# Reordering the first batches of a planned attention-and-FFN kernel: tiles A and B of the first batch ahead, the second batch's hold moved, the planner's transfer costs changed

## The chip, the cores and the metric

The kernel runs on one core of one Trainium2 chip. The core has TensorE (PE in the profile; PEld is its weight load), VectorE (DVE), ScalarE (ACT), GpSimd (POOL) and SyncE (SP), and 16 DMA engines. Each engine works through its own list of instructions strictly in order and waits on semaphores; SP and POOL also issue transfers from their lists. The metric is device time in microseconds, the median of the runs shown. Lower is better.

## The reference

Eight batches of eight heads, 576 queries, 576 keys plus 16 beacon keys that every query sees, 64 values per head. Causal attention is followed by a gated feed-forward network over the 4608 tokens:

```python
B, H, S, Nb, D = (8, 8, 576, 16, 64);  n_tokens, d_model, d_ff = (4608, 512, 1536)
k_all = concatenate([beacon_k, k], axis=2);  v_all = concatenate([beacon_v, v], axis=2)
scores = matmul(q, k_all.T) / sqrt(D)           # -1e9 where key > query; beacons always seen
a = exp(scores - scores.max(-1));  a /= a.sum(-1) + 1e-09
x = matmul(a, v_all)                            # to [B*S, H*D] = [4608, 512]
out = (maximum(x @ w_gate, 0) * (x @ w_val)) @ w_out
```

## The kernel before, in words

**A plan written out by a scheduler.** The program first makes a list of tasks (`add`), each with the engines that may do it, a cost in microseconds, the tasks it depends on, the buffers it holds (`Hold`) and a priority. `Plan.order` then plays the list through once: at every step it takes the task that can begin first, the smaller priority number winning among equals, and writes it behind the others on its engine. The result is a fixed order of instructions for each of the five engines. The costs are constants in the file: `c_dve`, `c_act`, `c_pool`, `c_pe` for the engines; for a transfer, an issue time and a time on "the wire", which is one common resource, and a fixed time behind it until it counts as landed (1.9). A different constant therefore changes no instruction by itself, but may change every order. The chip then runs these orders with its real durations, and an engine whose next instruction is not ready waits, whatever stands behind it.

**Fillers.** Where the plan sees TensorE idle before 160 us, it puts in matmuls that compute nothing (`fill`, line 987), one for each 0.1375 us of the gap (0.275 in the first ten microseconds; after 36 us only where a PSUM bank is free). They are part of TensorE's order for good.

**Attention.** Queries are cut into tiles of 64. For each batch, loads of q and k (lines 551, 576, 604) land in one of eight stage tiles `st`; they are rounded to bf16 `h` (line 511, on POOL or DVE for the first batch, on POOL for the others), turned by TensorE (line 522) and copied to kT and qT (lines 460, 462). v is loaded (lines 638 to 641) and copied to bf16 (line 464 or 462). A *quad* is four heads: its scores (line 740) go to PSUM, DVE adds the mask and takes the minimum of the negated scores (line 688), ACT does the exponential with its sum (line 695), DVE the reciprocal (line 701), POOL the normalisation (line 706). Then the probabilities are turned, for the first batch by TensorE (line 816), later by a DMA transpose (line 826), and multiplied with v (line 836). Query tiles are grouped in A, B (tiles 0 to 3 with their keys, 240 tokens), C, D, E (the other 320 tokens) and F (the last 16 tokens of all heads, lines 790 and 859). For the first batch A and B are a quad step of their own: their probabilities and the turned ones live in a part of the tile xT that is not yet needed, so in the profile the exponential and normalisation of A and B have the output `xT`, the others `pb`. The FFN can begin on the first 240 tokens when A and B of all eight heads are done.

**FFN.** Token spans of 240, 336, seven times 512, and 448. For each of twelve column blocks: four gate matmuls (line 897), ReLU on ACT (line 908), four value matmuls (line 902), product on DVE (line 913); then the output matmuls (line 928) by token tiles of 128, copied out of PSUM by DVE or ACT (460, 462) and stored by SP (line 942). At the end of the last span stands a tile of 64 tokens. It is computed as two column halves, the left on partitions 0 to 63 and the right on 64 to 127 **of the same PSUM bank**; the left half is copied by DVE or ACT and stored by SP, the right half copied and stored by ACT.

**Weights.** Nine transfers (three of w_gate, three of w_val, three of w_out), issued by POOL, each 4 x 128 rows by 512 columns, cast to bf16 on the way (line 474).

**What sets the order around the change.** The priorities: weights have -15, the loads of the first batch -20 (prio in `new_batch`), those of the second `RANK1`; the quads of the first batch 0 to 6, with `AB_FIRST` taken off for its A and B quads. `HELD` makes the loads of a batch, from a given place on, wait until a given weight transfer has been issued: a memset of one element on POOL (line 532) stands for the wait. Place 0 of the second batch is its rest rows of k, place 2 the first head pair's k, place 4 the second pair's.

## Time and profile before

| | us |
|---|---|
| median of 3 runs | 406.01 (405.50 to 406.61) |
| the profiled execution, its own time | 406.85 |
| its span | 404.8 |
| FFN matmuls, lines 897, 902, 928, busy | 104.7, 106.1, 99.1 |
| POOL normalisation, line 706, 272 | 142.1 |
| ACT exponential, line 695, 272 | 144.2 |
| DVE minimum, line 688, 288 | 134.3 |
| share of the 16 DMA engines: SP's queue, POOL's weights | 73.6%, 7.6% |

How to read it: busy times of lines add up per engine, and consecutive matmuls overlap in the records, so a line's sum may exceed its share of the time. A timeline row is start, duration, engine, line, operation, output and inputs, and in brackets the idle time of the engine just before and what ended it. A wait's row names who waited for whom. The share of the DMA engines can exceed 1 where their packets overlap. Times on POOL are rough.

### The profile page before, as it was taken

The numbers are of one execution on the slowest core, as the hardware profiler recorded it, in microseconds if no ns is written. First come the engines' busy times: TensorE is split into PE (matmuls) and PEld (weight loads), VectorE is DVE, ScalarE is ACT, GpSimd is POOL, SyncE is SP. The second block draws the span as 40 slices with busy tenths as digits, with TensorE's granted clock in tenths as the row PEclk, the third lists the DMA queues.
The fourth block names the chain that finished last, engine by engine and source line by source line (L and its number), as shares of the span: only waits on it lengthen the run. The fifth ranks groups of instructions, "written<-read, shape, count | busy, mean of one in ns | idle before, by whom it ended". The sixth has DMA issues, their size and how long they took to land.

```text
span 404.8 us, 9950 instructions
## 1 busy us (share of the span) xinstructions
PE 390.3 (96%) x3276; PEld 206.8 (51%) x3320; DVE 293.9 (73%) x1051; ACT 260.1 (64%) x809; POOL 234.7 (58%) x452
## 2 busy tenths in 40 slices
PE   7999999999999999999999899999999999999995
PEld 4667854655444545544455445454444454444542
DVE  3899798986977997769888977698777733442432
ACT  2989689768786786777776777588757721330320
POOL 6799779947395977567785768577565420000000
PEclk9999999999999999999999999999999999999999
DMA  7999997999999999959999999699948273001102
GB/s 179 215 193 216 240 223 147 185 206 204 203 202 217 236 187 275 185 161 189 254 181 201 228 230 177 171 255 226 172 78 175 42 147 123 0 0 53 52 2 91
DMA packets 174147, 67.99 MB, mean 168 GB/s; under 512 B 146384, under 2 KB 169552, under 8 KB 174096
## 3 DMA queue, kind: packets, MB, share of 16 engines
q1 hardware_dynamic: 169264, 62.57, 73.6%
q0 software_dynamic: 4752, 4.72, 7.6%
q8 instruction: 26, 0.43, 0.4%
q14 instruction: 25, 0.20, 0.2%
q10 hardware_dynamic: 80, 0.07, 0.1%
HBM read 38.54 MB, written 9.44 MB: 119 GB/s over the span
## 4 chain that ended last, share of the span: by engine, by line
PE 85%; DMA 5%; POOL 4%; DVE 2%; issue 2%; ACT 1%; SPq 1%; POOLq 0%; ACTq 0%; DVEq 0%
PE f L928 23%; PE f L902 22%; PE f L897 21%; PE f L740 6%; PE f L836 6%; PE f L522 4%; DMA wo_r<-in_moe_w_out_dram 2%; POOL xT L706 2%; DMA st<-in_v_dram 2%; PE f L816 1%; POOL pb L706 1%; PE f L987 1%; DMA st<-in_beacon_k_dram 1%; PE f L859 1%; PE f L790 1%
## 5 line engine op out<-in xcount | busy, mean ns | idle before, releaser
L706 POOL TENSOR_SCALAR pb<-pb,small 128x320 bf16<-128x320 bf16 (+8 forms) x272 | 142.1, 540 | 78.4 <-DVE small L701 73.5
L695 ACT ACTIVATE pb<-f,small 128x320 bf16<-128x320 f32 (+8 forms) x272 | 144.2, 553 | 22.7 <-DVE small L688 13.7
L688 DVE CUSTOM_DVE_ANT_0 f<-f,mask 128x320 f32<-128x320 f32 (+8 forms) x288 | 134.3, 517 | 12.1 <-PE f L740 7.2
L902 PE MATMUL f<-xT,wv_r 128*128 128x512 bf16 (+3 forms) x470 | 106.1, 358 | 0.5
L908 ACT ACTIVATE g<-f 128x512 f32<-128x512 f32 (+3 forms) x120 | 66.7, 565 | 60.6 <-PE f L897 53.8
L897 PE MATMUL f<-xT,wg_r 128*128 128x512 bf16 (+3 forms) x463 | 104.7, 357 | 0.9
L913 DVE TENSOR_TENSOR hT<-g,f 128x512 bf16<-128x512 f32 (+3 forms) x120 | 75.2, 632 | 38.1 <-PE f L902 34.7
L928 PE MATMUL f<-wo_r,hT 128*128 128x512 bf16 (+2 forms) x439 | 99.1, 374 | 1.9 <-issue 1.0
L897 PEld LDWEIGHTS <-wg_r 128*128 128x128 bf16 x480 | 45.3, 98 | 43.1 <-issue 1.2
L928 PEld LDWEIGHTS <-hT 128*128 128x128 bf16 (+2 forms) x456 | 41.9, 100 | 48.1 <-issue 4.0
L902 PEld LDWEIGHTS <-wv_r 128*128 128x128 bf16 x480 | 44.2, 98 | 42.3 <-issue 2.3
L695 ACT ACTIVATION_READ_ACCUMULATOR pb<-f,small 128x1 f32 x272 | 60.5, 222 | 0.0
L511 POOL TENSOR_SCALAR h<-st 128x512 bf16<-128x512 f32 (+1 forms) x92 | 48.6, 543 | 7.6 <-DMA st<-in_k_dram 3.1
L688 DVE DVE_READ_ACCUMULATOR2_ANT small<- 128x1 f32 x296 | 42.4, 143 | 0.2 <-issue 0.2
L740 PE MATMUL f<-kT,qT 64*64 64x64 bf16 (+7 forms) x640 | 35.9, 295 | 1.5 <-ACT pb L695 1.0
L462 DVE COPY osb<-f 128x512 f32<-128x512 f32 (+2 forms) x26 | 17.7, 681 | 24.0 <-PE f L928 24.0
L701 DVE RECIPROCAL small<-small 128x2 f32<-128x2 f32 (+3 forms) x144 | 22.1, 163 | 14.1 <-ACT pb L695 9.3
L522 PE MATMUL f<-ident,h 128*128 128x128 bf16 (+1 forms) x320 | 27.9, 219 | 2.5 <-POOL h L511 1.4
L522 PEld LDWEIGHTS <-h 128*128 128x128 bf16 (+1 forms) x320 | 21.0, 99 | 15.6 <-POOL h L511 5.8
L740 PEld LDWEIGHTS <-qT 64*64 64x64 bf16 x640 | 15.1, 106 | 23.9 <-issue 18.5
L836 PE MATMUL f<-pTb,v 128*64 128x320 bf16 (+3 forms) x488 | 26.0, 253 | 0.0
L836 PEld LDWEIGHTS <-v 128*64 128x64 bf16 (+1 forms) x512 | 20.6, 109 | 9.7 <-issue 7.2
(60 smaller groups left out, 236.0 us busy)
## 6 DMA issues: line engine op xcount, KB each, us to landing
out_dram<-osb SPq DMA_DIRECT2D x34, 256.0 KB, 2.2
st<-in_k_dram SPq DMA_DIRECT2D x32, 256.0 KB, 4.6
st<-in_q_dram SPq DMA_DIRECT2D x32, 256.0 KB, 5.1
st<-in_v_dram SPq DMA_DIRECT2D x24, 256.0 KB, 5.8
st<-in_v_dram SPq DMA_DIRECT2D x8, 224.0 KB, 6.3
wg_r<-in_moe_w_gate_dram POOLq DMA_DIRECT2D x3, 512.0 KB, 6.2
wv_r<-in_moe_w_val_dram POOLq DMA_DIRECT2D x3, 512.0 KB, 6.6
wo_r<-in_moe_w_out_dram POOLq DMA_DIRECT2D x3, 512.0 KB, 7.7
```

The source lines that it names most:

```text
L511: (nc.gpsimd if x.engine == "POOL" else nc.vector).tensor_scalar(to, src, by, 1.0, ALU.mult, ALU.mult)
L522: nc.tensor.matmul(to, h16.tile[:rows, a * P:(a + 1) * P], ident[:rows, :rows], start=True, stop=True)
L688: nc.vector.tensor_tensor_reduce(out=view(i, n - m), in0=view(i, n - m), in1=msk, scale=1.0, scalar=at(7) if m < n else 3.0e38, op0=ALU.ad ...
L695: nc.scalar.activation(ph.tile.rearrange("p a n -> p (a n)")[:, a:a + n], view(i), AF.Exp, bias=at(i), scale=-1.0, accum_out=at(4 + i))
L706: nc.gpsimd.tensor_scalar(one, one, at(8 + i), 1.0, ALU.mult, ALU.mult)
L740: nc.tensor.matmul(banks[k][b_].tile[64 * i:64 * i + 64, off:off + n], t.q.tile[r, 2 * g + i, 64 * j:64 * j + 64], t.kT.tile[r, 2 * g + i, ...
L836: nc.tensor.matmul(ps.tile[64 * hh:64 * hh + 64, d0:d0 + w], t.v.tile[:rows, c, D * h:D * h + D], rhs(64 * hh), start=(c == 0), stop=(c == ...
L897: nc.tensor.matmul(psg.tile[:, :mt], wg_r[:, ki, nf * P:(nf + 1) * P], xT[:, ki, m0:m0 + mt], start=(ki == 0), stop=(ki == KM - 1))
L902: nc.tensor.matmul(psv.tile[:, :mt], wv_r[:, ki, nf * P:(nf + 1) * P], xT[:, ki, m0:m0 + mt], start=(ki == 0), stop=(ki == KM - 1))
L908: r = add("ACT", c_act(mt), lambda _, psg=psg, g=g: nc.scalar.activation(g.tile[:, :mt], psg.tile[:, :mt], AF.Relu), (a,), (psg, g), -1000 ...
L913: hid.append(add("DVE", c_dve(mt), lambda _, psv=psv, g=g, nf=nf: nc.vector.tensor_mul(hT[nf].tile[:, :mt], g.tile[:, :mt], psv.tile[:, :m ...
L928: nc.tensor.matmul(ps.tile[64 * c:64 * c + rows, :w], hT[nf].tile[:, t0:t0 + rows], wo_r[:, nf, w * c:w * c + w], start=(nf == 0), stop=(n ...
```

## The change

It touches constants of the plan and one detail of the last tile.

- `AB_FIRST` 40 instead of 0: the A and B quads of the first batch get priorities of -40 to -38 instead of 0 to 2.
- `RANK1` -14 instead of -19: the priority of the second batch's loads.
- `HELD`: the second batch's first place is no longer held; its third place (first head pair) waits for the first transfer of w_val instead of the third of w_gate; its fifth place waits for the third of w_val as before.
- The planner's cost of a weight on the wire is 0.70 instead of 0.78 per 128 x 512 block, of v 1.25 instead of 1.54, and the time to landing 1.8 instead of 1.9.
- The last tile's two halves each hold a PSUM bank.

```diff
-RANK1 = -19.0
+RANK1 = -14.0
-HELD = {(1, 0): ("v", 0, 0), (1, 2): ("g", 0, 1024), (1, 4): ("v", 0, 1024)}
+HELD = {(1, 2): ("v", 0, 0), (1, 4): ("v", 0, 1024)}
-AB_FIRST = 0
+AB_FIRST = 40
+W_MOVE = 0.7
+V_MOVE = 1.25
+LAND = 1.8
...
-                end = max(wire, free[e]) + 1.9
+                end = max(wire, free[e]) + LAND
...
-                    end = wire + 1.9
+                    end = wire + LAND
...
-            d[...], s[...]), (), (), work, 0.1, move=0.78 * kos * w / 512,
+            d[...], s[...]), (), (), work, 0.1, move=W_MOVE * kos * w / 512,
...
-            ld = add("DMA", (1.1 if c == 0 else 0.55, 1.54 * rows / P), fetch, (held,), (st,), prio[0])
+            ld = add("DMA", (1.1 if c == 0 else 0.55, V_MOVE * rows / P), fetch, (held,), (st,), prio[0])
...
-            ps, osb = Hold(f_s, 4 if halves == 1 else 3), [Hold(osb_s, 2) for _ in range(halves)]
+            ps, osb = [Hold(f_s, 4 if halves == 1 else 2) for _ in range(halves)], [Hold(osb_s, 2) for _ in range(halves)]
...
-                            nc.tensor.matmul(ps.tile[64 * c:64 * c + rows, :w], hT[nf].tile[:, t0:t0 + rows],
+                            nc.tensor.matmul(ps[c].tile[64 * c:64 * c + rows, :w], hT[nf].tile[:, t0:t0 + rows],
...
-                ev = add("ACT" if c else ("ACT", "DVE"), {...}, evict, (prev,), (ps, osb[c]), -1000 + prio)
+                ev = add("ACT" if c else ("ACT", "DVE"), {...}, evict, (prev,), (ps[c], osb[c]), -1000 + prio)
```

What the built programs then issue, engine by engine, is the same work in another order. POOL's list from the fifth cast to the sixth weight, in words (line numbers of before; "norm AB" is line 706 with output xT, "norm C.." with output pb):

```
before                                   after
cast h (k, second quad, first half)      cast h (same)
cast h (q, same)                         weight wg 1
cast v0, cast v1                         cast v0, cast v1, cast h (k, first quad, second half)
norm AB x6                               norm AB x16
weight wg 1
norm AB x2, cast v2
weight wv 1                              weight wv 1
norm AB x1, memset (hold), norm AB x7    weight wg 2, memset (hold)
norm C.. x1, weight wg 2                 norm C.. x2, weight wv 2
norm C.. x4, weight wv 2                 cast h (k rest, second batch), norm C.. x3, weight wg 3
norm C.. x5, weight wg 3                 norm C.. x2, weight wv 3
```

TensorE's list (matmuls of each kind ahead of the place named):

| ahead of | fillers | turns, line 522 | scores, line 740 | gate, value |
|---|---|---|---|---|
| first gate matmul, before | 76 | 40 | 52 | 0, 0 |
| first gate matmul, after | 62 | 40 | 44 | 0, 0 |
| first value matmul, before | 82 | 40 | 56 | 12, 0 |
| first value matmul, after | 74 | 44 | 48 | 12, 0 |
| first gate matmul of the third span, before | 103 | 108 | 200 | 96, 96 |
| first gate matmul of the third span, after | 91 | 124 | 200 | 96, 96 |

No filler stands behind the last place in either. At the last place all other kinds are equal.

More of the change, by code (lines that the diff above doesn't have):

```diff
@@ L474, in weight @@
         x = add("POOL", W_ISSUE, lambda t: nc.gpsimd.dma_start(
-            d[:, ko:ko + kos, n0:n0 + w], s[:, ko:ko + kos, n0:n0 + w]), (), (), work, 0.1, move=0.78 * kos * w / 512,
+            d[:, ko:ko + kos, n0:n0 + w], s[:, ko:ko + kos, n0:n0 + w]), (), (), work, 0.1, move=W_MOVE * kos * w / 512,
             after=W0 + W_STEP * len(weight_in) / KM)
@@ L933, in ffn, with evict @@
                     need += hid[:11]
-                prev = add("PE", k * c_pe(w) + SWITCH * (halves - 1), outp, need, (ps,) + tuple(hT[k * part:k * part + k]),
+                prev = add("PE", k * c_pe(w) + SWITCH * (halves - 1), outp, need, tuple(ps) + tuple(hT[k * part:k * part + k]),
                            prio + 0.3 + 0.01 * part - (0.5 if part else 0))
             for c in range(halves):
-                def evict(x, c=c, ps=ps, osb=osb[c], rows=rows, w=w):
+                def evict(x, c=c, ps=ps[c], osb=osb[c], rows=rows, w=w):
                     copy(x.engine, osb.tile[64 * c:64 * c + rows, :w], ps.tile[64 * c:64 * c + rows, :w])
@@ L942, in store @@
                     q_.dma_start(out[m0 + t0:m0 + t0 + rows, w * c:w * c + w], osb.tile[64 * c:64 * c + rows, :w])
-                ev = add("ACT" if c else ("ACT", "DVE"), {"ACT": c_act(w), "DVE": c_dve(w)}, evict, (prev,), (ps, osb[c]), -1000 + prio)
+                ev = add("ACT" if c else ("ACT", "DVE"), {"ACT": c_act(w), "DVE": c_dve(w)}, evict, (prev,), (ps[c], osb[c]), -1000 + prio)
                 add("DMA", (0.4, 0.78 / halves), store, (ev,), (osb[c],), prio + OUT)
```

## The prediction

> **What bounds the kernel now.** I read, in this order, the busy time of each engine and the slices, the waits of TensorE, its timeline up to the first FFN matmuls, GpSimd's timeline over the same stretch, the landing times of the transfers, and the last six microseconds.
>
> ```profile
> PE 390.3 (96%) x3276; PEld 206.8 (51%) x3320; DVE 293.9 (73%) x1051; ACT 260.1 (64%) x809; POOL 234.7 (58%) x452
> ...
> PEclk9999999999999999999999999999999999999999
> ...
> L987 PE MATMUL f<-mask,ident x103: 269/273/421, 2.0 to 93.3; 128*128 128x256 bf16 x103
> ```
>
> TensorE is busy 390.3 of 404.8 us. The fourteen idle ones are 2.9 in the first five microseconds, about four behind the last matmul, and some seven between. So the total work of TensorE sets the end, and the useful part of it is the same in both kernels. What can change is the fillers (103 matmuls of line 987, all of them dummies), the waits, and the tail. The waits that the profile can name are few (what waited, for whom; us in total, times, longest):
>
> ```profile
> PE f L740 <- ACT pb L695: 1.0, 2, 0.8
> PE f L522 <- ACT pb L695: 1.0, 1, 1.0
> ...
> PE f L928 <- DMA wo_r<-in_moe_w_out_dram: 0.3, 1, 0.3
> ```
>
> The opening stage is a different matter. There GpSimd is the engine without a pause, and weights are issued between its normalisations:
>
> ```profile
> 11.11 0.62 POOL L464 TENSOR_SCALAR v<-st 128x512 bf16<-128x512 f32 x1 [1.12 <-DMA st<-in_v_dram]
> ...
> 13.73 2.85 POOL L706 TENSOR_SCALAR xT<-xT,small 128x64 bf16<-128x64 bf16 x6 [0.97 <-DVE small L701]
> 16.52 0.94 POOL L474 DMA_DIRECT2D wg_r<-in_moe_w_gate_dram  x1
> 17.50 0.93 POOL L706 TENSOR_SCALAR xT<-xT,small 128x256 bf16<-128x256 bf16 x2
> ...
> 18.98 0.79 POOL L474 DMA_DIRECT2D wv_r<-in_moe_w_val_dram  x1
> 19.82 0.55 POOL L706 TENSOR_SCALAR xT<-xT,small 128x64 bf16<-128x64 bf16 x1
> ...
> 20.39 2.98 POOL L706 TENSOR_SCALAR xT<-xT,small 128x64 bf16<-128x64 bf16 x7
> ```
>
> ```profile
> 25.45 0.58 PE L897 MATMUL f<-xT,wg_r 128*128 128x240 bf16 x4
> ...
> 27.94 1.39 PE L902 MATMUL f<-xT,wv_r 128*128 128x240 bf16 x12
> ```
>
> Start, duration, instruction, and in brackets what it waited for. The sixteen normalisations of A and B (output xT) take 2.85 + 0.93 + 0.55 + 2.98 = 7.3 us but run from 13.7 to 23.4, since two weight issues and a cast of v stand among them. The gate matmuls follow at 25.45, the value matmuls at 27.94. The end:
>
> ```profile
> 400.55 0.42 DVE L462 COPY osb<-f 64x256 f32<-64x256 f32 x1 [0.74 <-PE f L928]
> 401.00 0.37 ACT L460 COPY osb<-f 64x256 f32<-64x256 f32 x1 [9.87 <-DVE osb L462]
> 401.40 0.56 ACTq L942 DMA_DIRECT2D out_dram<-osb  x1
> ```
>
> ScalarE's copy of the last tile's right half starts only when VectorE's copy of the left half, out of the same bank, is done.
>
> **The change, part by part.** *New constants (W_MOVE, V_MOVE, LAND, AB_FIRST, RANK1)* issue nothing by themselves; they re-sort all five queues. What they do is read from the order of the built programs.
>
> *Fillers.* 91 instead of 103. Up to the first gate matmul there are 62 instead of 76, with 8 score matmuls less as well; from there to the end 29 instead of 27. Fourteen of them in a row took 1.70 us (from 11.61), the last one's latency included, so 0.11 us each: 12 x 0.11 = 1.3 us off the engine that sets the end. **-1.3**.
>
> *Last tile in two banks.* ScalarE's copy then needs only its own matmuls and can start with VectorE's, 0.45 us earlier. The left half's store is issued at 401.0 and lands 2.0 us later whatever the right half does, so the end moves by the distance between the two stores, 401.40 - 401.0 = 0.4 us. The second bank is one that the tile before last gave back at 398.1, and the last tile's matmuls start at 399.0, so taking it costs nothing; had it to wait for the last full tile's copy (until 399.8) it would cost 0.8. **-0.4**.
>
> *First gate weights.* Their issue moves on GpSimd's queue from between the A and B normalisations to right behind the fifth cast, about 8.9 us, into the 1.12 us that GpSimd idles before the first v. That takes 0.94 us off GpSimd's chain. But there it meets the first batch's own loads. Those landed 3.0 to 4.1 us after issue at the start and 4.8 to 6.7 from 6.2 us on, since the DMA engines' packets add up to 1.2 to 1.3 of their time (they overlap) from 9 to 16 us. The k load issued at 7.36 landed after 5.6 us, at 13.0. Its cast moves from VectorE to GpSimd, ahead of the normalisations, and if it lands late all of them wait behind it; the q load's cast, in VectorE's queue, holds up the reciprocals behind it likewise. What a weight transfer beside them costs is bounded by the loads that had one: those issued at 20.4 to 22.4 took 5.0 to 5.7 us, the like one at 16.3, before any weight moved, 3.6; so 1.4 to 2.1 us. The lower end is nothing (the loads are ahead in time); the upper end is a weight transfer's whole time on the wires, 7.6% of the span for nine, 3.4 us each. I take 1.
>
> *A and B first.* The sixteen normalisations then stand together, and the first value weights, issued at 18.98 before, stand behind them; so do all later weights. Undisturbed they end at 13.7 + 7.3 = 21.0 instead of 23.4. The value weights are issued 2.1 us later than before and land 6.6 us after issue, as before: 27.7. TensorE has 8 fillers and 8 score matmuls less (0.9 + 0.7 us) and four turns more (0.3) ahead of its first value matmul, so it gets there at 27.94 - 1.3 = 26.6 and waits 1.1 us for them. With the 1 us of the paragraph before it waits 2.1, with 3.4 us 4.5; with none of it and weights that land in the shortest time seen, 5.7, 0.2. **+2.0**.
>
> *Held loads.* The second batch's rest rows no longer wait, the hold starts at its first head pair, one memset of 0.09 us goes, and the third batch's rest rows of k (cast 0.78 us on GpSimd, 0.56 on VectorE, all before 42 us) move behind. By the first 512-wide gate matmul, TensorE has done sixteen turns of later batches more (1 us of later work) and all else as before. The output weights stand ten to fifteen places earlier on GpSimd's queue (third issue 57.53 before), so their 0.33 us wait goes. The waits in this stretch were 0.23, 0.20, 0.81 and 0.33 us: work piles up behind the late value weights, so I take them as gone. **-1.6**; if new ones of the same size replace them, 0. Of the waits behind 95 us (0.97 and 0.41 us for the second to fifth batch's rounding) a third, since loads are further ahead: **-0.4**, between 0 and -1.4.
>
> *SP's queue* has as many entries as before; the second pair of transposes now stands behind five loads. The first transpose took its place at 70.04 and four took 17.03 us, so a load that waits for a stage tile there could hold them; GpSimd's normalisations for the first pair come seven instructions (3 us) earlier, which covers that.
>
> **Sum.** -1.3 - 0.4 + 2.0 - 1.6 - 0.4 = -1.7 us. The profiled execution took 406.85 us (span 404.8 and 2.05 around it), 0.84 above the median 406.01. So 405.15 for such a run, and **404.3** for a median.
>
> [...]
>
> **The rivals.**
> - *The wait for the value weights eats what the fillers gave* (no change). They decide when the wait passes 2.5 us and the later waits half remain: -1.3 - 0.4 + 2.6 - 0.8 = +0.1, 406.1. For it: the issue stands behind 7.3 us of work that can't be moved. Against: the plan filled this gap already, 12 fillers between the first gate and value matmuls.
> - *The first batch's loads lose the wires* (slower). The k load lands 3.4 us late, at 16.4; GpSimd, strictly in order, starts normalising 2.7 to 3.4 us late; value weights land at 31, the next ones 3 us apart behind them, and TensorE waits 4.5. Old waits stay: -1.3 - 0.4 + 4.5 - 0.5 = +2.3, 408.3. It decides from 3.5 us of delay. For it: the wires are at 1.2 and more from 9 to 16 us, and idle (0.71 to 0.76) from 16 to 19, where the first weights start now. Against: loads beside weights at 32.3 us took 4.8 and 5.1, less than the 5.6 of the crowded start. [...]
> - *A clock that drops.* The granted clock is 1.00 in every stretch, and no wait after the start is over 1 us; a wait of 4.5 would be new. If the matmuls behind it ran at half rate for 3 us it would add 1.5, to 409.8. [...]
>
> That the change does not put A and B first is excluded: the built order has the sixteen normalisations without a weight among them.
>
> **How the numbers follow.** A median of three here varies by about 0.3% (405.5 to 406.61), 1.2 us, which is what I call no change. Forecast 0.45, its own range 402.5 to 404.8; no change 0.28; loads that lose the wires 0.22; the clock or an unknown wait in the re-sorted later stages 0.05. That gives faster 0.45, same 0.28, slower 0.27. The unknowns run from -1.3 - 0.4 + 0.2 - 1.6 - 1.4 = -4.5 to +2.8; the 80% range leaves out a tenth on either side: 402.3 to 408.3.
>
> **What would show it.** Right: first gate matmul near 23.5 us, first value matmul at 27.5 to 29 behind a wait for wv_r; 91 fillers; ScalarE's last copy starting with VectorE's; first 512-wide gate matmul near 93.5 (94.70 now). Wrong: the cast of the second k half on GpSimd after 15 us with a wait for its load; TensorE waits over 3 us before 36 us; or TensorE idle over 4 us between 95 and 400.

## The result, and the profile after

The changed kernel takes **409.69 us** (median of ten runs, 407.54 to 412.34) against 406.03 (ten runs, 404.56 to 408.08): **1.009 of the kernel before, 95% interval 1.0063 to 1.0118**. It is slower by 0.9%, 3.7 us, where the prediction had 404.3. The profiled execution took 407.96 us, with a span of 406.3. A run more than 1.5% above the fastest of its kernel counts as slow and is left out of the ratios.

The first lines of the page of the changed kernel, and its list of TensorE's waits (what waited, for whom; us in total, times, longest):

```profile
PE 388.5 (96%) x3266; PEld 204.5 (50%) x3308; DVE 291.1 (72%) x1041; ACT 263.1 (65%) x820; POOL 234.4 (58%) x450
```

```profile
PE f L525 <- ACT xT L698: 2.3, 1, 2.3
PE f L900 <- DMA wg_r<-in_moe_w_gate_dram: 2.3, 1, 2.3
...
PE f L905 <- DMA wv_r<-in_moe_w_val_dram: 0.9, 2, 0.5
```

TensorE is busy 1.8 us less than before (twelve fillers less). By later profiles of the same two orders it is 0.9 us less, 393.6 and 392.7: they hold 3320 and 3308 matmul records, these two lack some forty each. But two waits of 2.3 us are new; the kernel before had none over 1.0 behind the first five microseconds. The first is between 14 and 16.5 us, the second at 30.3 to 32.6. GpSimd's timeline of the changed kernel (start, duration, instruction; in brackets the idle time before it and what ended it):

```profile
8.77 0.94 POOL L477 DMA_DIRECT2D wg_r<-in_moe_w_gate_dram  x1
...
13.94 2.11 POOL L709 TENSOR_SCALAR xT<-xT,small 128x64 bf16<-128x64 bf16 x6 [0.46 <-DVE small L704]
16.61 0.94 POOL L709 TENSOR_SCALAR xT<-xT,small 128x256 bf16<-128x256 bf16 x2 [0.56 <-DVE small L704]
18.62 3.54 POOL L709 TENSOR_SCALAR xT<-xT,small 128x64 bf16<-128x64 bf16 x8 [1.08 <-DVE small L704]
22.11 0.79 POOL L477 DMA_DIRECT2D wv_r<-in_moe_w_val_dram  x1
22.90 0.75 POOL L477 DMA_DIRECT2D wg_r<-in_moe_w_gate_dram  x1
```

The first gate weights are issued 7.75 us earlier than before, the first value weights 3.1 us later (18.98 before). What the early transfer met is the load of the second quad's q, issued right behind it. The size and the time from issue to landing, before and then in the changed kernel:

```profile
st<-in_q_dram SPq DMA_DIRECT2D x1, 256.0 KB, 5.0
```

```profile
st<-in_q_dram SPq DMA_DIRECT2D x1, 256.0 KB, 7.1
```

VectorE's timeline of the changed kernel:

```profile
16.02 0.43 DVE L514 TENSOR_SCALAR h<-st 128x512 bf16<-128x512 f32 x1 [2.11 <-DMA st<-in_q_dram]
```

This is the cast of that q: VectorE stood still for 2.11 us for its load, and the turn of that q is TensorE's wait at 14 to 16.5 (the list of waits names ScalarE, which had long been done). The second wait, in TensorE's timeline:

```profile
24.32 0.58 PE L900 MATMUL f<-xT,wg_r 128*128 128x240 bf16 x4
...
27.70 1.40 PE L905 MATMUL f<-xT,wv_r 128*128 128x240 bf16 x12
...
32.58 1.40 PE L900 MATMUL f<-xT,wg_r 128*128 128x240 bf16 x12 [2.28 <-DMA wg_r<-in_moe_w_gate_dram]
...
35.57 0.58 PE L905 MATMUL f<-xT,wv_r 128*128 128x240 bf16 x4 [0.38 <-DMA wv_r<-in_moe_w_val_dram]
```

The first value matmul does not wait at all: its weights landed at 27.64, just in time, and TensorE came there 0.24 us earlier than before. It is the **second** gate weights that are late: issued at 22.90 (0.9 us earlier than before), they took 9.6 us instead of 6.7, right behind the value weights. What the wires did meanwhile, in one-microsecond stretches of the changed kernel (the last three columns: granted clock, share of the DMA engines, GB/s):

```profile
19.00:20.00 1.00, 1.00 (x18) 0.73 (x16) 1.00 (x6) 1.00 (x4) 1.00 (x5) 1.00 0.51 117
...
22.00:23.00 1.00, 0.78 (x11) 0.56 (x11) 0.39 (x1) 0.68 (x2) 1.00 (x3) 1.00 0.64 134
23.00:24.00 1.00, 1.00 (x20) 0.69 (x23) 1.00 (x5) 0.71 (x2) 1.00 (x3) 1.00 0.34 17
...
25.00:26.00 1.00, 0.98 (x11) 0.75 (x9) 1.00 (x5) 1.00 (x4) 0.96 (x2) 1.00 1.23 203
```

From 19 to 25 us they were half idle (0.34 to 0.85, where the kernel before had 1.03 to 1.26), because all weights but one stood behind the sixteen normalisations (with the value weights alone moved back among them, below, the same stretch is at 1.16 to 1.39); from 25 us on they were full (1.16 to 1.25 in every microsecond up to 43), and the weights landed 3.0 to 3.7 us apart (32.5, 35.5, 39.0, 42.7). The end went as forecast:

```profile
401.89 0.42 DVE L465 COPY osb<-f 64x256 f32<-64x256 f32 x1 [0.74 <-PE f L931]
401.92 0.37 ACT L463 COPY osb<-f 64x256 f32<-64x256 f32 x1 [9.44 <-PE f L931]
402.32 0.57 ACTq L945 DMA_DIRECT2D out_dram<-osb  x1
```

ScalarE's copy starts 0.03 us behind VectorE's. But the two stores now meet: the left one took 2.3 us to land instead of 2.0. From the start of VectorE's last copy to the last landing it is 2.73 us instead of 2.89.

The two profiled executions differ less (1.5 us of span) than the medians (3.7): that of the kernel before was 0.8 us above its median, that of the changed kernel 1.7 below.

### The profile page after: what moved, and what is told of

It reads as the page before. It is cut to its first block, busy times and chain, and to the rows that moved or that the text cites. A ratio compares the mean times of both kernels' runs of the same rounds, so it can differ in the third digit from the quotient of the medians.

```text
span 406.3 us, 9963 instructions
## 1 busy us (share of the span) xinstructions
PE 388.5 (96%) x3266; PEld 204.5 (50%) x3308; DVE 291.1 (72%) x1041; ACT 263.1 (65%) x820; POOL 234.4 (58%) x450
## 4 chain that ended last, share of the span: by engine, by line
PE 84%; DMA 6%; DVE 4%; POOL 2%; issue 1%; ACT 1%; SPq 0%; DVEq 0%; POOLq 0%; ACTq 0%
PE f L931 23%; PE f L905 22%; PE f L900 21%; PE f L743 6%; PE f L839 5%; PE f L525 4%; DMA wv_r<-in_moe_w_val_dram 3%; DMA st<-in_q_dram 3%; DVE f L691 1%; PE f L819 1%; POOL pb L709 1%; POOL xT L709 1%; DMA st<-in_k_dram 1%; PE f L862 1%; PE f L793 1%
## 5 line engine op out<-in xcount | busy, mean ns | idle before, releaser
L691 DVE CUSTOM_DVE_ANT_0 f<-f,mask 128x64 f32<-128x64 f32 (+8 forms) x288 | 134.2, 513 | 10.6 <-PE f L743 6.8
L931 PE MATMUL f<-wo_r,hT 128*128 128x512 bf16 (+3 forms) x437 | 98.6, 374 | 1.6 <-issue 1.0
L931 PEld LDWEIGHTS <-hT 128*128 128x128 bf16 (+3 forms) x456 | 41.8, 100 | 46.4 <-issue 2.9
L691 DVE DVE_READ_ACCUMULATOR2_ANT small<- 128x1 f32 x296 | 41.5, 140 | 0.0
L465 DVE COPY osb<-f 128x512 f32<-128x512 f32 (+3 forms) x29 | 19.8, 681 | 25.6 <-PE f L931 25.2
L743 PE MATMUL f<-kT,qT 64*64 64x512 bf16 (+7 forms) x640 | 35.2, 292 | 0.2
L467 POOL TENSOR_SCALAR v<-st 128x512 bf16<-128x512 f32 (+1 forms) x37 | 22.6, 619 | 9.2 <-DMA st<-in_v_dram 8.4
```

Of the source, the lines that this page charges most:

```text
L691: nc.vector.tensor_tensor_reduce(out=view(i, n - m), in0=view(i, n - m), in1=msk, scale=1.0, scalar=at(7) if m < n else 3.0e38, op0=ALU.ad ...
L743: nc.tensor.matmul(banks[k][b_].tile[64 * i:64 * i + 64, off:off + n], t.q.tile[r, 2 * g + i, 64 * j:64 * j + 64], t.kT.tile[r, 2 * g + i, ...
L931: nc.tensor.matmul(ps[c].tile[64 * c:64 * c + rows, :w], hT[nf].tile[:, t0:t0 + rows], wo_r[:, nf, w * c:w * c + w], start=(nf == 0), stop ...
```

## The experiments

Ratios are to the kernel before on the same chip, with 95% intervals; 0.1% is 0.4 us. Where an order is edited behind the planner, this stands in place of the last loop, so that one instruction moves on one engine and nothing is planned anew:

```python
seq = plan.order()
norms = [t for t in seq if not isinstance(t, Filler) and t.run.__qualname__.endswith("norm") and t.engine == "POOL"]
def ahead(x, y):          # x right in front of y
    seq.remove(x); seq.insert(seq.index(y), x)
```

| kernel | ratio | interval |
|---|---|---|
| changed, again | 1.0083 | 1.0051 to 1.0115 |
| before, two banks | 0.9983 | 0.9958 to 1.0008 |
| changed, both waits filled | 1.0113 | 1.0073 to 1.0153 |
| changed, value weights among normalisations | 1.0017 | 0.9988 to 1.0046 |
| changed, first gate weights among them | 1.0073 | 1.0046 to 1.0100 |
| changed, both among them | 1.0034 | 1.0016 to 1.0052 |
| changed, AB_FIRST 0 | 1.0116 | 1.0080 to 1.0151 |
| changed, old HELD and RANK1 | 1.0234 | 1.0206 to 1.0263 |
| changed, value weights among, first wait filled | 1.0055 | 1.0023 to 1.0086 |
| before, 57 fillers less | 1.0016 | 0.9991 to 1.0041 |
| before, two banks, output weights earlier | 0.9975 | 0.9945 to 1.0005 |
| the same, again | 0.9978 | 0.9957 to 0.9999 |
| changed, AB_FIRST 0, first gate weights among | 1.0006 | 0.9986 to 1.0026 |
| changed, value and second gate weights among | 1.0026 | 1.0004 to 1.0049 |
| before, two banks, new HELD and RANK1 | 1.0044 | 1.0023 to 1.0066 |
| before, two banks, new transfer costs | 1.0249 | 1.0208 to 1.0290 |
| before, two banks, 4.4 us of fillers at 95 us | 1.0117 | 1.0083 to 1.0152 |
| changed, both among, 4.4 us of fillers at 95 us | 1.0099 | 1.0066 to 1.0133 |

### The clock: the changed kernel again, fillers in its waits, fillers out of the kernel before

*The changed kernel again*, no edit.

> The changed kernel itself, unaltered, for a second profile and more runs. In its first profile, taken at a granted clock of 1.00, TensorE stands idle 9.8 us before 45 us against 4.1 before the change, and the run took 407.96 us; the median of its ten runs is 409.69, and in seven of them the mean clock was 0.985 to 0.995. Theory 1 (waits, and then the clock): the long waits cost about 1.5 us of the span, and in part of the runs the clock drops behind one of them, which costs the other 2 to 4. Then runs with a clock of 1.00 lie near 407.7, the others at 409.5 to 412, and a profile of such a run shows a stretch of a few microseconds with a clock well below 1 behind a wait of over 2 us (13.9 to 16.5, or 30.3 to 32.6). Theory 2 (the clock has nothing to do with it): time and clock do not go together, and no stretch of the profile shows a lower clock.

Of the first ten runs and the eleven of these that count, nine had a mean clock of 0.996 or more (407.0 to 409.6 us, mean 408.2) and twelve less (407.8 to 412.4, mean 410.8). So time and clock go together; which drives which is not told by that. This profile (408.34 us) again has two long waits, 1.7 us each, at the same places.

*Both waits filled.*

```diff
+    at = {round(t.prio, 4): j for j, t in enumerate(seq) if not isinstance(t, Filler) and t.engine == "PE"}
+    for j in (at[1000.08], at[-19.91]):
+        seq.insert(j, Filler(20, fill_bank, fill))
```

> The changed kernel with twenty fillers (0.11 us each, 2.2 us) put into TensorE's list ahead of each of its two long waits: ahead of the turn of the first batch's second q, first half, (idle 13.9 to 16.5) and ahead of the gate matmuls of the second weight transfer (idle 30.3 to 32.6). No other engine's list changes, and both waits end when they ended, since what they wait for is a transfer. Theory 1 (the clock drops behind the waits): TensorE stays busy, the clock is 1.00 in all runs, and the median falls from about 409.7 to 407.7 or 408, though 4.4 us of work that computes nothing were added. Theory 2 (the clock has nothing to do with it): no change within 0.5 us, 409.5. A third possibility, that the fillers are late themselves and push the work behind them: 410 to 412.

411.07 us, mean clocks 0.994 to 1.000: the clock was back (0.998 on average) and the time was not. The third possibility came out, so a full clock alone does not bring the time back. More this run cannot say, since the fillers were themselves in the way: in its profile the q load landed at 13.39, with no wait, and the turn of q began only behind the first twenty fillers, at 16.35; the second gate weights landed at 32.02, and their matmuls began behind the second twenty, at 32.86.

*The kernel before without 57 fillers* between 9 and 25 us.

```diff
+        if isinstance(t, Filler) and j < first:   # first: index of the first gate matmuls; 19 fillers kept
+            if skip <= 0:
+                continue
+            skip -= t.n
```

> The kernel before without the 57 fillers that stand in TensorE's list between 9 and 25 us (fillers compute nothing; all results stay). It opens short idle gaps of 0.3 to 1.7 us in that stretch, 6 us together, with nothing else moved. If fillers lie on the path that sets the end (the prediction's step, 0.11 us each): up to 6 us faster, at least 1. If they are hidden, since TensorE waits for transfers and for the other engines in that stretch anyway: no change at a clock of 1.00. By the clock theory the gaps drop the clock to 0.50 for some microseconds in most runs: clock 0.985 to 0.995, and 1 to 4 us slower, though nothing but dummies was taken away.

This settles the clock for the order of the kernel before. All twelve runs had a mean clock of 0.979 to 0.990, and the time is that of the kernel before, +0.16% (interval -0.09 to +0.41, so +0.6 us, 1.0 either way). Stretches of this run's profile, with the granted clock in the third column from the right:

```profile
14.00:15.00 1.00, 0.20 (x4) 0.03 (x1) 1.00 (x6) 1.00 (x7) 1.00 (x3) 1.00 1.28 269
15.00:16.00 1.00, 0.58 (x6) 0.41 (x7) 0.81 (x5) 1.00 (x4) 1.00 (x4) 0.68 1.25 214
16.00:17.00 1.00, 0.84 (x8) 0.40 (x7) 0.38 (x2) 1.00 (x5) 0.95 (x3) 0.50 1.04 195
...
24.00:25.00 1.00, 1.00 (x16) 0.76 (x16) 1.00 (x6) 0.51 (x2) 0.96 (x2) 0.50 1.29 261
25.00:26.00 1.00, 1.00 (x10) 0.64 (x9) 0.98 (x5) 0.85 (x3) 1.00 (x3) 0.70 1.06 128
```

For ten microseconds TensorE ran at half rate, and its first gate matmul still began at 25.31 (25.45 before), its first value matmul at 27.91 (27.94):

```profile
25.31 0.71 PE L897 MATMUL f<-xT,wg_r 128*128 128x240 bf16 x4
...
27.91 1.29 PE L902 MATMUL f<-xT,wv_r 128*128 128x240 bf16 x11
```

In this stretch TensorE is not what the work waits for. It follows as well that the fillers there lie beside other work: 57 of them gone are worth nothing within 1 us. For the changed order there is one pair of profiles: with the gate weights alone put back (below) the clock was 0.50 for 3.4 us from 19.6 on, and the first gate and value matmuls began at 24.50 and 27.88; with both weights back (the value weights' place is then another too) and a clock of 1.00 at 24.44 and 27.82. So the lower clock did not show there either, up to that point. What it costs the changed kernel itself was not measured.

*Value weights among the normalisations, first wait filled* (the next section's edit and the first of the two groups of fillers above).

> The changed kernel with the value weights' issue between the eighth and ninth normalisation of A and B (as in the run before, 407.3 us, whose mean clock was 0.990 to 0.995 in half its runs), and with twenty fillers put into TensorE's list ahead of the turn that waits for the second q half between 14 and 16. In profiles that caught it, the granted clock falls to 0.50 between 16 and 24 us, for 3 to 6.5 us, behind an idle stretch of 1.5 to 3 us of TensorE. Clock theory: with that stretch filled the clock is 1.00 in all runs, and the time is that of the undisturbed ones of the run before, 405.4 to 406.4, 405.9 in the middle. Against it (the clock is a sign of late transfers and costs nothing itself, as the changed kernel with both waits filled suggests, where the clock was 1.00 and the time 411): 407.3 or more.

Ratio 1.0055, against 1.0017 without the fillers. The clock was 0.996 or more in ten of twelve runs; the time was not lower. But again the fillers were in the way: in this profile the q load landed at 13.38, and the turn of q began behind them, at 16.92. So this run does not decide on the clock. That the low clocks of the changed order are a sign of late transfers fits these runs; it is argued, not shown.

### The weights' places on GpSimd's list

*Value weights back among the normalisations.*

```diff
+    ahead(weight_in["v", 0, 0], norms[8])
```

> The changed kernel with the issue of the first value weights moved on GpSimd's list to between the eighth and the ninth normalisation of A and B, where it stood in the kernel before; all else is that of the changed kernel. Theory A (the wires stand idle from 19 to 25 us since all weights but the first are behind the sixteen normalisations, and every later weight lands 3 us apart behind them): the value weights are issued near 17.7 instead of 22.1 and land by 24, the second gate weights land near 29.5 instead of 32.5, TensorE's wait of 2.28 us for them goes to nothing, and the time falls by 1.5 to 2.3 us, more if the clock is spared as well. The first gate matmul comes up to 0.8 us later, as the last eight normalisations wait for the issue. Theory B (the loss is the first batch's loads that meet the first gate weights, 2 us late at q): the wait at 13.9 to 16.5 stays, the second one shrinks, and the time falls by under 1 us.

1.0017 instead of 1.0083 to 1.009: 0.7% back, 2.7 us with 1.7 either way. They were issued at 16.60, and the gate matmuls on the second gate weights began at 31.25 with no wait. TensorE's timeline of this run:

```profile
28.65 1.40 PE L905 MATMUL f<-xT,wv_r 128*128 128x240 bf16 x12
...
31.25 1.45 PE L900 MATMUL f<-xT,wg_r 128*128 128x240 bf16 x12
```

Theory A; the size is a little above the upper end of what it gave, and within the uncertainty.

*First gate weights back alone*, and *both*.

```diff
+    ahead(weight_in["g", 0, 0], norms[6])
```

> The changed kernel with the issue of the first gate weights alone moved back on GpSimd's list, from in front of the first v to between the sixth and the seventh normalisation of A and B, where it stood before; the value weights stay behind the sixteenth. Theory B (these weights meet the first batch's own loads): the second q half lands near 14 instead of 15.9 us and TensorE's idle 2.2 to 2.4 us between 13.5 and 20 go to under 0.5. If that wait were worth its length, the time falls by about 2 us, to 408. Theory A (what counts is when the value weights and the second gate weights are issued): TensorE only reaches the wait for the second gate weights earlier and waits there that much longer, so the time falls by no more than the value weights are issued earlier, 0.6 us: 409.2 to 410.

> The changed kernel with both first weights back among the normalisations of A and B on GpSimd's list: the gate weights behind the sixth, the value weights behind the eighth. All other lists are those of the changed kernel. Moving the value weights alone gave 407.3 us, with 2.0 us of TensorE's idle time left between 13.5 and 20. If the two causes add up, that idle time goes too: 405.3 to 405.6, at or below the kernel before. If the first wait is only passed on to the next (the weights still land 3 us apart), 406.5 to 407.3. A danger of its own: the gate weights land at 16.6 + 6.2 = 22.8 and the value weights behind them near 26.5, 1.5 us later than TensorE wants them.

Alone 1.0073, both 1.0034. With them back, VectorE's cast of q no longer waited for its load, but of the time 0.1 to 0.2% came back, within the uncertainty: the wait was passed on. TensorE's idle time between 13.5 and 20 did not go under 0.5 but stayed at 1.75 us, now 1.52 of it for normalisations that stand behind the weights' issue, and 1.5 us for the second gate weights were left. Both together are no better than the value weights alone.

*Second gate weights among them too.*

```diff
+    ahead(weight_in["v", 0, 0], norms[8])
+    ahead(weight_in["g", 0, 512], norms[12])
```

> The changed kernel with the first value weights' issue between the eighth and ninth and the second gate weights' between the twelfth and thirteenth normalisation of A and B. If the place of the weights' issues is all that the changed order loses: the second gate weights land by 28.5, no wait for a weight over 0.5 us is left, and the ratio to the kernel before falls from 1.0017 to 0.997 to 1.000. If another 0.8 us of issue within the normalisations delays the first gate matmul as much as it gains: 1.001 to 1.004.

1.0026: the second expectation. It is no better than the value weights alone.

### The parts of the change, alone and undone

*AB_FIRST back to 0 in the changed kernel.*

```diff
-AB_FIRST = 40
+AB_FIRST = 0
```

> The changed kernel with AB_FIRST at 0 as before; the planner re-sorts everything. On GpSimd's list the first gate weights stay in front of the first v, the value weights stand behind the seventh normalisation, the second gate weights behind the tenth. Theory A (A and B first puts the weights behind sixteen normalisations, and that is most of the loss): most of the loss goes, 406 to 407.5, and TensorE's wait for the second gate weights is under 0.5 us. Theory B (the first gate weights beside the first loads): their wait stays, 408 to 409.5.

1.0116: not better but, if anything, worse. So A and B first is not by itself what makes the kernel slow. The same kernel with the gate weights put back:

```diff
-AB_FIRST = 40
+AB_FIRST = 0
...
+    ahead(weight_in["g", 0, 0], norms[6])
```

> The changed kernel with AB_FIRST at 0 (409.6 us, TensorE idle 3.2 us between 13.5 and 20 and the clock at 0.50 from 17.4 to 23.9) and, besides, the first gate weights' issue moved back on GpSimd's list behind the sixth normalisation. If the gate weights beside the first loads are what makes the first loads late and the clock drop (theory B, through the new transfer costs, which brought this issue forward): idle time between 13.5 and 20 under 1 us, clock 1.00, 405.5 to 407. If it is the order of the rest that costs: 409 to 410.

1.0006, the time of the kernel before. One transfer, moved on one queue behind ten other instructions, was worth 1.1%, 4.5 us with 1.7 either way. GpSimd's timeline of the first of the two kernels,

```profile
8.63 1.10 POOL L477 DMA_DIRECT2D wg_r<-in_moe_w_gate_dram  x1
...
16.89 0.62 POOL L514 TENSOR_SCALAR h<-st 128x512 bf16<-128x512 f32 x1 [3.50 <-DMA st<-in_q_dram]
17.48 2.26 POOL L709 TENSOR_SCALAR xT<-xT,small 128x64 bf16<-128x64 bf16 x6
```

and of the second:

```profile
13.96 0.62 POOL L514 TENSOR_SCALAR h<-st 128x512 bf16<-128x512 f32 x1 [0.25 <-DMA st<-in_q_dram]
14.65 2.27 POOL L709 TENSOR_SCALAR xT<-xT,small 128x64 bf16<-128x64 bf16 x6
16.88 0.94 POOL L477 DMA_DIRECT2D wg_r<-in_moe_w_gate_dram  x1
```

Here the q cast stands on GpSimd ahead of the normalisations; beside the weights its load lands 2.9 us later (16.71 against 13.79), the first six normalisations begin 2.8 us later, and the normalisations and weight issues behind them 2.5 to 2.6.

*Transfer costs alone*, on the kernel before with two banks.

```diff
+W_MOVE = 0.7
+V_MOVE = 1.25
+LAND = 1.8
```

> The kernel before with the last tile in two banks and, of the change, only the three transfer costs. The plan then issues the first gate weights in front of the first v and the value weights behind the seventh normalisation, as in the changed kernel with AB_FIRST at 0, which took 1.0116 of the kernel before. If the gate weights beside the first loads are a cost of their own (theory B): TensorE idle 2.5 to 4 us between 13.5 and 20 us, ratio 1.008 to 1.013. If that loss needed the new hold as well: 0.997 to 1.003.

**1.0249**, 416.59 us: the three constants cost 2.7% by themselves, more than either expectation. The profile has TensorE idle 3.7 us between 13.5 and 20, the first gate matmul at 33.13 (25.45 before) and the first 512-wide one at 101.17 (94.70); from there to the end it takes 314.2 us (310.1 before). How much of this is the gate weights' place, and how much the rest of the new order and its fillers (131 instead of 103), is not separated.

*HELD and RANK1 alone*, on the kernel before with two banks, and *undone* in the changed kernel.

```diff
-RANK1 = -19.0
+RANK1 = -14.0
-HELD = {(1, 0): ("v", 0, 0), (1, 2): ("g", 0, 1024), (1, 4): ("v", 0, 1024)}
+HELD = {(1, 2): ("v", 0, 0), (1, 4): ("v", 0, 1024)}
```

> The kernel before with the last tile in two banks and, of the change, only RANK1 and HELD; transfer costs and AB_FIRST as before. On GpSimd's list the first six weights keep their places among the normalisations up to the second value weights; the output weights come earlier (third at 50.9 instead of 57.7 by the plan). By the prediction's step on held loads and old waits (-1.6 and -0.4): 2 us faster than with two banks alone, a ratio to the kernel before of 0.993. By the reading of the runs so far (that step is worth nothing): 0.997 to 1.001.

> The changed kernel with RANK1 and HELD of the kernel before, so that the second batch's loads are ranked and held as they were. The lists up to the first value weights are those of the changed kernel; behind 22 us the planner re-sorts, and puts 132 fillers in instead of 91. By the prediction's step on the held loads (worth 1.6 us): the waits between 45 and 95 us come back, 1.5 us more idle there, 411 to 412. If instead the second batch's loads, issued unheld from 18.9 us on, take the wires from the weights: the second gate weights land earlier than 32 us and the time falls to 408 or less. If the 41 fillers more are not all hidden they add up to 4.5 us.

Alone 1.0044, that is 0.6% (2.5 us) slower than two banks alone. Undone in the changed kernel 1.0234, 1.4% worse than with it. The first is slower than both expectations, and so is the second unless the fillers named there count. The new hold costs time with the old transfer costs and saves some with the new ones: the parts do not add. In both the planner re-sorts the rest and puts other fillers in (124 and 132), so neither is the hold alone.

*Two banks alone*, the kernel before with only the last tile's edit.

```diff
-            ps, osb = Hold(f_s, 4 if halves == 1 else 3), [...]
+            ps, osb = [Hold(f_s, 4 if halves == 1 else 2) for _ in range(halves)], [...]
```

> The kernel before with one part of the change, the last tile in two banks; no other instruction moves. By the prediction's step: ScalarE's last copy starts with VectorE's, the end comes 0.4 us earlier, so 405.6. By the profile of the changed kernel, where the two stores are issued together at about 402.3 and the left one takes 2.3 instead of 2.0 us to land: 0.1 to 0.2 us earlier or nothing, 405.8 to 406.0. By the theory that a late wait is what lowers the clock: the runs here all have a clock of 1.00, since the first 95 us are those of the kernel before.

405.54 us, 0.17% faster, with an interval that includes no change; both expectations lie in it. In its profile it is 2.77 us from the start of VectorE's last copy to the last landing, 0.1 less than before. Its profile also has a wait that the first profile of the same order showed with 0.3 us:

```profile
64.79 1.02 PE L928 MATMUL f<-wo_r,hT 128*128 128x512 bf16 x4 [1.59 <-DMA wo_r<-in_moe_w_out_dram]
```

*Output weights eight to ten places earlier*, with two banks, run twice.

```diff
+    for ko, back in ((0, 8), (4, 10), (8, 8)):
+        x = weight_in["o", ko, 0]
+        ahead(x, pool[pool.index(x) - back])      # pool: GpSimd's tasks in order
```

> The kernel before with the last tile in two banks and the three output weights issued eight, ten and eight places earlier on GpSimd's list (in the kernel before, the third issue at 57.5 us, and TensorE waits for it 0.3 us in one profile and 1.6 in the other, near 63 us); nothing else moves. By the prediction's step on the held loads and output weights: that wait goes, 0.3 to 1.6 us off the kernel with two banks, so 0.4 to 0.7% faster than the kernel before. Against it: the transfers only compete earlier with the last value weights, whose wait then comes in its place: same as with two banks, 0.2% faster.

> The kernel before with the last tile in two banks and the three output weights issued earlier, a second time (0.9975 of the kernel before, interval 0.9945 to 1.0005). If it is faster: 0.996 to 0.998 again, and the stretch from the first 512-wide gate matmul to the end at 308 to 309 us. If the first result was chance: 0.999 to 1.001.

0.9975 and 0.9978: the fastest order of this study, 0.2% ahead of the kernel before (only the second interval, 0.9957 to 0.9999, excludes no change) and about 1% ahead of the changed one. The wait for wo_r is gone from both profiles, but the gain on two banks alone is within the uncertainty.

### The later stages

*Forty fillers ahead of the first 512-wide gate matmul*, on the kernel before with two banks and on the changed kernel with both weights back.

```diff
+    seq.insert(at[1020.0], Filler(40, seq[at[1020.0]].holds[0].tile, fill))
```

> The kernel before with the last tile in two banks and forty fillers (0.11 us each, 4.4 us) in TensorE's list right ahead of the first 512-wide gate matmul, near 95 us. The sum of the prediction takes TensorE's work as what sets the end, so that each microsecond there counts in full: then the time rises by 4.2 to 4.6 us, to a ratio of 1.009 to 1.010. If TensorE waits for the other engines behind 95 us by as much as its profile shows (2 to 4 us idle, part of it for rounding), the delay lets them get ahead and costs 1 to 3 us: 1.001 to 1.006.

> The changed kernel with both first weights back among the normalisations (1.0034 of the kernel before) and forty fillers, 4.4 us, ahead of the first 512-wide gate matmul. On the order of the kernel before the same fillers cost 1.3%, 5.4 us with an uncertainty of 1.5: the whole of them. If the later stages of the changed order wait for other engines in small pieces: less than 3 us, a ratio of 1.006 to 1.011, and the stretch from the first 512-wide gate matmul to the end falls from 310.5 to 309 or less. If TensorE's own work is what is longer: 4 to 5 us, 1.013 to 1.016, and that stretch stays at 310 to 311.

On the first order they cost 1.34% (1.0117 against 0.9983), 5.4 us with 1.7 either way: a delay at 95 us reaches the end in full. On the second 0.65% (1.0099 against 1.0034), 2.6 us with 1.5 either way. By the time, part of the delay is absorbed there; but the stretch behind it did not shrink in that run's profile. Not settled.

The stretch from the first 512-wide gate matmul to the end, in all profiles that share one of two TensorE orders from there on:

| TensorE's order | first 512-wide gate matmul, us | from there to the end, us |
|---|---|---|
| before (six profiles: before, two banks, fewer fillers, output weights twice, delay) | 94.70, 96.22, 96.03, 95.11, 94.55, 100.37 | 310.1, 308.6, 309.3, 308.1, 308.6, 308.2 |
| changed (nine: changed twice, waits filled, value weights, gate weights, both, one wait filled, three weights, delay) | 96.94, 96.05, 96.34, 95.06, 96.06, 94.23, 96.23, 95.39, 100.48 | 309.3, 310.6, 311.1, 310.5, 310.2, 310.5, 311.9, 310.0, 310.4 |

By the first pair alone, before and changed, the later stretch looks shorter after the change. Over all profiles it is 308.8 against 310.5 us: **1.7 us longer**, though sixteen turns (1 us) had moved ahead of it. The runs were on several chips; on each of the four that ran both orders after the first pair, the changed one is longer, by at least 1.8 us.

Part of it can be read from the profiles. Some lack about forty matmul records of this stretch, and a missing record looks like idle time. In those that lack none, TensorE has no idle time at all between 100.5 and 390 us in the order before (two profiles), and 0.5 to 1.6 us in the changed one (four), most of it ahead of turns that wait for casts of later batches on GpSimd. That is about 1 of the 1.7 us; the rest stays open.

## Why the prediction was wrong, point by point

The step that failed is the sum's use of TensorE's own work as what sets the end in the opening too, where the fillers that go had stood. There other engines and the transfers set the pace, so the gain of 1.3 us was not there; nor was that of 1.6 for the held loads. The loss sat at the second gate weights, whose wait the sum does not have.

- **Fillers, -1.3: failed.** The step counted each filler less as 0.11 us off the engine that sets the end. In the opening TensorE does not set it: 57 fillers less changed nothing (+0.6 us, 1.0 either way), and even half the clock for 10 us left the first FFN matmuls where they were. The change drops fourteen fillers in this stretch and adds two later. The premise itself, that TensorE sets the end, holds behind 95 us in the order before, where 4.4 us of fillers cost 5.4 (1.7 either way).
- **Last tile in two banks, -0.4: mechanism right, size not resolved.** ScalarE's copy starts with VectorE's, and alone the edit gives -0.7 us, 1.0 either way; by the profiles it gives 0.1 to 0.2. The sum left out that the left store, issued together with the right one, would land later: it took 2.3 us instead of 2.0, in the changed kernel and with two banks alone.
- **First gate weights among the first loads, 1 us: right in kind, too small.** The step priced k's load and named q's beside it. That k came in time (cast at 12.86, as the prediction's own test asked), but the q load issued beside the weights took 7.1 us instead of 5.0, and the four loads behind it 8.4 to 9.9 instead of 4.8 to 6.7: 2.1 to 3.5 us more, nearer to the step's upper end of 3.4 than to the 1 it took. (The load that it took as free of weights, issued at 16.26, was still under way when weights were issued at 16.52.) In the changed order the wait is mostly passed on (0.1 to 0.2%); with AB_FIRST at 0 the same transfer costs 1.1%. The transfer costs alone cost 2.7%, and of what they do the prediction priced only the weights' places in the final order.
- **Wait for the weights, +2.0: place wrong, and the size right by luck.** Putting the value weights back is worth 2.7 us. But the sum had TensorE at the first value matmul at 26.6, 1.3 us earlier for its smaller list, and waiting there; it came at 27.70, when the weights had just landed, and did not wait. The wait was at the second gate weights, which the sum does not have: value and gate weights now stand back to back on the wires, which the half-idle stretch before had not used.
- **Held loads and old waits gone, -1.6: the waits went, the gain did not come.** Between 45 and 95 us TensorE's idle time did go, from 1.7 to 0.2 us. But the waits had moved ahead: 9.8 us idle before 45 us instead of 4.1. The new hold and rank alone make the kernel before 2.5 us slower (1.3 either way); undone in the changed kernel they cost 1.4%. So their sign hangs on the rest of the order, and no run shows the gain of 1.6.
- **Waits behind 95 us, -0.4: failed.** The 0.97 and 0.41 us that a third was to be taken from are in one profile of this order only; the five others have 0 to 0.2 us. There was nothing to take. The idle time of this stretch, too, was mostly not there: the profile before lacks 44 matmul records, and one of the same order that lacks none has 3.3 us more busy time. The stretch became 1.7 us longer. Its named waits in the changed order are 0 to 1.3 us in eight of nine profiles (2.2 in the ninth, all for casts of later batches on GpSimd): where the step took time away, the change put some in. That explains about 1 us; why the rest of the stretch is longer stays open.
- **The rivals.** "The first batch's loads lose the wires" was the nearest, at 408.3: loads late by the gate weights, following weights 3 us apart, TensorE waiting 4.5 us (4.6 in the two long waits). It erred in the load and in the place of the wait, and in keeping the gains of fillers and tail, so that its time came near is in part luck. "A clock that drops" happens, in most runs of the changed kernel (a mean of 0.985 to 0.995 in seven of its first ten), but no run shows it costing time; in the changed order itself that was not measured. No run shows the 1.5 us that this rival adds for 3 us at half rate: the runs show a clock of 0.50 for 3.42 to 10.24 us, and the one with 10.24, without 57 fillers, took 0.6 us more than the kernel before, 1.0 either way.

So of the 3.7 us, 2.7 (1.7 either way) were the place of the value weights (shown), up to 0.8 the first gate weights (not resolved in this order), and the gains that were to outweigh them did not exist. The 1.7 us of the later stretch are seen in the profiles and not in this sum; with both weights back 0.34% (1.4 us) remain, which they could be. That is argued, not shown.

## What to carry to other kernels

Before counting a dummy or a saved instruction as time, find out whether its engine sets the pace in that very stage: take a handful away, or look whether work behind them starts earlier. When a transfer is issued earlier, ask which small loads on the critical chain it will meet; when one is issued later, ask for the next ones as well: here they landed 3.0 to 3.7 us apart. A planner's constants are not harmless because they issue nothing: try each alone, and read a wait as standing only when a second profile of the same order shows it too.

## What the runs showed of the hardware

- **The clock was at half rate for one, two or three times 3.4 us.** In the run with 57 fillers less, the rows give 0.64 + 9 + 0.60 = 10.24 us at a granted clock of 0.50 (twice the missing share of each microsecond); with AB_FIRST at 0, 6.84; with the gate weights alone put back, 3.42: three, two and one times 3.41 to 3.42. The length of a gap alone does not tell whether the clock falls: in the last case TensorE was busy for 0.27, 0.20 and 1.00 of the three microseconds from 16 to 19, idle 1.5, and the clock fell between 19 and 20; in the profile of the changed kernel a gap of 2.34 us left it at 1.00.
- **Loads issued behind a weight transfer landed about 3 us later.** In two kernels that differ in this one place the q load landed at 13.79 us without it and at 16.71 with it. Over all twenty profiles: where the gate weights are issued near 9 us (nine), the next four loads behind q took 8.1 to 10.3 us to land, where they are issued later (eleven) 4.6 to 7.5. The q load itself, issued within 0.7 us of the weights, varied: it took 6.0 to 8.1 us in six of the nine and 4.4 to 4.5 in three, where the others have 4.2 to 5.0. What makes this delay no run shows.
